# The last 64 rows of a 448-row contraction as two 64-row tiles side by side, in an attention kernel on one core

## The chip, the cores and the metric

The kernel runs on one core of a Trainium2 chip. The metric is the device time of one execution in microseconds, lower is better. A "slot" below is the distance from one matmul's start to the next in an unbroken stream.

## The reference

Two independent attention blocks (A and B) share one form. Each has 16 batches, 144 queries, a model width of 448, 16 heads of width 256, and a key/value cache of 512 positions:

```python
q = (x @ wq).reshape(B, Sq, H, Dh).transpose(0, 2, 1, 3)       # contraction over 448
scores = einsum("bhqd,bhkd->bhqk", q, k_cache) * Dh ** -0.5
p = softmax(scores)
o = einsum("bhqk,bhkd->bhqd", p, v_cache)
out = o.transpose(0, 2, 1, 3).reshape(B, Sq, H * Dh) @ wo
```

One batch and head is a "unit"; there are 2 x 16 x 16 = 512 of them. The contraction of Q is over 448 rows, which is three and a half times the 128 rows of TensorE. That half is what the change is about.

## The kernel before

A Python scheduler issues one step of the pipeline per unit and puts semaphores between the engines. Here are the parts that matter, with cuts marked and short comments added. The fourth chunk of the Q contraction (`kc == 3`) holds 64 rows of zeros, written once, above the 64 rows of real weights, and so runs as a full 128-row matmul.

```python
# PSUM tiles: eight banks in all
qp_ps = ps("qp_ps", [128, 512], F32)                                  # 1 bank: Q of one head, 2 x 144 columns
s_ps = [ps("s_ps%d" % i, [128, 2, 512], F32) for i in range(2)]       # 4 banks: scores, two units in flight
ot_ps = [ps("ot_ps%d" % i, [128, 512], F32) for i in range(2)]        # 2 banks: PV and the row sums
op_ps = ps("op_ps", [128, 512], F32)                                  # 1 bank: output projection
# ... (cut)
def t_q(U):
    pr, b, h = unit(U)
    XG = (pr * Bn + b) // XB
    xsl = XG % NXG
    xo = (b % XB) * SQ
    hg = h // 4

    def e(t):
        ins = None
        for kc in range(4):
            for dc in range(2):
                c0 = h * DH + dc * 128
                ins = t.matmul(qp_ps[:, dc * SQ:(dc + 1) * SQ], lhsT=wq_sb[:, kc, c0:c0 + 128],
                               rhs=xt_sb[:, xsl, kc, xo:xo + SQ], start=(kc == 0 and dc == 0),
                               stop=(kc == 3), skip_group_check=True)
        return ins
    S.add(PE, e, reads=[(("wq", hg), pr), ("wqz", 0), (("xt", xsl), XG)], writes=[("qp", ("q", U))],
          banks=["qp"], name="Q%d" % U)

def t_evac_q(U):
    sl = U % NQT
    src = qp_ps[:, 0:2 * SQ].rearrange("p (c q) -> p c q", c=2)

    def e(v):
        return v.tensor_copy(qt_sb[:, sl, :, :], src)
    S.add(DVE, e, reads=[("qp", ("q", U))], writes=[(("qt", sl), U)], banks=["qp"], name="eq%d" % U)

def t_s(U):
    G, jj = divmod(U, UG)
    ksl = G % NK
    bank = U % 2

    def e(t):
        ins = None
        for c in range(4):
            for dc in range(2):
                ins = t.matmul(s_ps[bank][:, c // 2, (c % 2) * SQ:(c % 2 + 1) * SQ],
                               lhsT=kt_sb[:, 2 * c + dc, (ksl * UG + jj) * 128:(ksl * UG + jj + 1) * 128],
                               rhs=qt_sb[:, U % NQT, dc, :], start=(dc == 0), stop=(dc == 1))
        return ins
    S.add(PE, e, reads=[(("qt", U % NQT), U), (("kt", ksl), G)], writes=[(("sp", bank), U)],
          banks=["s%d" % bank], name="S%d" % U)

def t_exp(U):
    bank = U % 2
    psl = U % NPT

    def e(a):
        return a.activation(pt_sb[:, psl, :, :].rearrange("p (a b) q -> p a (b q)", a=2),
                            s_ps[bank][:, :, 0:2 * SQ], AF.Exp, scale=DH ** -0.5)
    S.add(ACT, e, reads=[(("sp", bank), U)], writes=[(("pt", psl), U)], banks=["s%d" % bank], name="ex%d" % U)

# ... (cut) one step of the main loop; LQ = 6, LS = 2
u = i + LQ
if 0 <= u < NT:
    t_q(u); t_evac_q(u)          # PE: 8 matmuls; DVE: PSUM to SBUF
u = i + LS
if 0 <= u < NT:
    t_s(u); t_exp(u); t_presum(u)  # PE: 8 matmuls; ACT: exp; POOL: sums of exps
u = i
if 0 <= u < NT:
    t_pv(u); t_sum(u)            # PE: 8 + 1 matmuls
    t_recip(u); t_check(u); t_evac_ot(u)   # ACT, DVE, DVE
# ... (cut) then 0 to 12 (once 32) pieces of the output projection, 128x448 matmuls
```

The whole kernel:

## Time and profile before

The time before is 1112.46 us (median of three, 1112.11 to 1113.15).

| quantity | value | view |
|---|---|---|
| PE busy | 1044.0 of 1112.2 us | the page, part 1 |
| slot of a 128x144 matmul | 62.5 ns | timeline: eight take 0.50 us |
| slot of a 128x448 matmul | 188.5 ns | timeline |
| sum of all slots | 12,800 x 62.5 ns + 1,152 x 188.5 ns = 1017 us | worked out |
| PE gaps ahead of Q, waiting for the evacuation | 79 of about 0.27 us, 21 us | single records; waits |
| PE pauses over 1 us after the first matmul | 24.6 us in all | single records |

First the page of the kernel before: its span, its busy times, and some groups. In a group's line the numbers after the bar are busy us, mean ns of one instruction, and idle time before it with what ended it.

```profile
span 1112.2 us, 33041 instructions
...
PE 1044.0 (94%) x13952; PEld 920.7 (83%) x13952; DVE 657.3 (59%) x2183; ACT 620.2 (56%) x1573; POOL 642.2 (58%) x1065
...
L975 ACT ACTIVATE pt_sb<-s_ps 128x576 bf16<-128x576 f32 x512 | 332.9, 650 | 452.2 <-PE s_ps L963 452.1
...
L939 PE MATMUL qp_ps<-xt_sb,wq_sb 128*128 128x144 bf16 x4096 | 346.2, 228 | 52.7 <-DMA wq_sb<-in_A_wq_dram 32.5
...
L951 DVE CAST qt_sb<-qp_ps 128x288 bf16<-128x288 f32 x512 | 225.4, 440 | 101.4 <-PE qp_ps L939 98.0
```

TensorE is the bound. The mean of 228 ns for a matmul is a modelled, pipelined length, not what a matmul costs. That has to be read from the distance between starts. The next lines are the timeline of PE before the change, in a step that carries two pieces of the output projection (start us, length us, then the merged instructions):

```profile
505.39 0.66 PE L939 MATMUL qp_ps<-xt_sb,wq_sb 128*128 128x144 bf16 x8
505.89 0.66 PE L963 MATMUL s_ps<-qt_sb,kt_sb 128*128 128x144 bf16 x8
506.39 0.66 PE L1009 MATMUL ot_ps<-pt_sb,v_sb 128*128 128x144 bf16 x8
```

Eight Q matmuls start at 505.39, the eight of S at 505.89 and the eight of PV at 506.39, so each group takes 0.50 us, or 62.5 ns a matmul. Nothing lies between the groups. In steps without output projection the picture is different:

```profile
70.52 0.23 PE L1021 MATMUL ot_ps<-ps_sb,ones 128*128 128x144 bf16 x1
70.84 0.68 PE L939 MATMUL qp_ps<-xt_sb,wq_sb 128*128 128x144 bf16 x8
```

The row-sum matmul starts at 70.52, so its slot ends at 70.58, but Q starts only at 70.84. Every second Q shows this gap of about 0.26 us. The waits view names its cause (what waited, for whom, total us, times, longest us):

```profile
PE qp_ps L939 <- DMA wq_sb<-in_A_wq_dram: 32.5, 2, 22.7
PEld qp_ps L939 <- DVE qt_sb L951: 26.4, 83, 0.8
PE qp_ps L939 <- DMA wq_sb<-in_B_wq_dram: 9.6, 1, 9.6
...
PE s_ps L963 <- DMA kt_sb<-in_A_k_cache_dram: 3.2, 1, 3.2
```

The Q matmuls of a unit have to wait until DVE has emptied the single Q bank of the unit before. The other lines are the pauses for loads: wq at the start and at the change to block B, and K once.

### The profile page before, as it was taken

How to read it: one execution, taken by the hardware profiler on the slowest of the kernel's cores; microseconds unless marked ns; L12 is line 12 of the kernel's file. 1: busy time of each engine (PE TensorE's matmuls, PEld its weight loads, DVE VectorE, ACT ScalarE, POOL GpSimd, SP SyncE). 2: the span in 40 equal slices, each digit the busy share in tenths (PEclk: the TensorE clock that was granted, in tenths of full speed). 3: DMA queues.
4: the chain of work that ended last, by engine and by line, in shares of the span. 5: the costliest groups of instructions: out<-in, count | busy, mean ns of one | idle time of the engine just before them, and what ended most of it. 6: DMA issues, size and time to landing. Idle time of an engine off the chain costs nothing.

```text
span 1112.2 us, 33041 instructions
## 1 busy us (share of the span) xinstructions
PE 1044.0 (94%) x13952; PEld 920.7 (83%) x13952; DVE 657.3 (59%) x2183; ACT 620.2 (56%) x1573; POOL 642.2 (58%) x1065
## 2 busy tenths in 40 slices
PE   1698999999999999999969999999999999999995
PEld 0597888888888888898858888888888888888884
DVE  1364666666656666666636656666666666666653
ACT  0364555666655555665535555566665555566552
POOL 0364656666656656666636656666665665666652
PEclk9898999999999999999989999999999999999998
DMA  9999999999999999999999999999999999999930
GB/s 251 292 301 304 301 241 273 269 275 287 288 242 263 269 275 258 249 309 277 276 271 313 279 279 280 278 274 269 316 268 271 253 273 285 266 275 259 272 88 12
DMA packets 626399, 294.19 MB, mean 265 GB/s; under 512 B 547776, under 2 KB 555968, under 8 KB 626240
## 3 DMA queue, kind: packets, MB, share of 16 engines
q1 hardware_dynamic: 624512, 287.85, 105.0%
q0 software_dynamic: 1728, 4.13, 1.3%
q8 instruction: 111, 1.82, 0.6%
q14 instruction: 48, 0.39, 0.1%
HBM read 148.90 MB, written 4.13 MB: 138 GB/s over the span
## 4 chain that ended last, share of the span: by engine, by line
PE 76%; DVE 8%; ACT 6%; SPq 4%; DMA 4%; issue 1%; POOLq 0%; POOL 0%; ACTq 0%
PE qp_ps L939 20%; PE s_ps L963 19%; PE op_ps L1100 19%; PE ot_ps L1009 16%; ACT pt_sb L975 4%; SPq L914 3%; DVE run_sb L1065 3%; DVE ring L1052 2%; DVE qt_sb L951 2%; PE ot_ps L1021 2%; DMA kt_sb<-in_A_k_cache_dram 2%; ACT ln_sb L1032 1%; DMA wo_sb<-in_B_wo_dram 1%; DMA wq_sb<-in_A_wq_dram 1%; DMA wq_sb<-in_B_wq_dram 0%
## 5 line engine op out<-in xcount | busy, mean ns | idle before, releaser
L984 POOL TENSOR_TENSOR pp_sb<-pt_sb 128x288 f32<-128x288 bf16 x512 | 373.5, 730 | 415.9 <-ACT pt_sb L975 414.8
L975 ACT ACTIVATE pt_sb<-s_ps 128x576 bf16<-128x576 f32 x512 | 332.9, 650 | 452.2 <-PE s_ps L963 452.1
L1065 DVE TENSOR_REDUCE run_sb<-ot_ps 1x1 bf16<-1x144 f32 x1024 | 262.2, 293 | 342.2 <-ACT ln_sb L1032 342.2
L939 PE MATMUL qp_ps<-xt_sb,wq_sb 128*128 128x144 bf16 x4096 | 346.2, 228 | 52.7 <-DMA wq_sb<-in_A_wq_dram 32.5
L939 PEld LDWEIGHTS qp_ps<-xt_sb,wq_sb 128*128 128x128 bf16 x4096 | 282.8, 99 | 127.2 <-issue 42.8
L963 PE MATMUL s_ps<-qt_sb,kt_sb 128*128 128x144 bf16 x4096 | 343.0, 227 | 3.2 <-DMA kt_sb<-in_A_k_cache_dram 3.2
L1009 PE MATMUL ot_ps<-pt_sb,v_sb 128*128 128x144 bf16 x4096 | 341.7, 227 | 0.0
L951 DVE CAST qt_sb<-qp_ps 128x288 bf16<-128x288 f32 x512 | 225.4, 440 | 101.4 <-PE qp_ps L939 98.0
L963 PEld LDWEIGHTS s_ps<-qt_sb,kt_sb 128*128 128x128 bf16 x4096 | 277.2, 99 | 4.1 <-DMA kt_sb<-in_A_k_cache_dram 3.4
L1009 PEld LDWEIGHTS ot_ps<-pt_sb,v_sb 128*128 128x128 bf16 x4096 | 276.0, 98 | 0.4
L988 POOL TENSOR_TENSOR ps_sb<-pp_sb 128x144 bf16<-128x144 f32 x512 | 250.0, 488 | 40.1
L1100 PE MATMUL op_ps<-wo_sb,ring 128*128 128x448 bf16 x1120 | 264.9, 353 | 1.3 <-DMA wo_sb<-in_B_wo_dram 0.8
L1052 DVE TENSOR_TENSOR ring<-ot_ps,rinv_sb 128x288 bf16<-128x288 f32 (+8 forms) x640 | 231.1, 375 | 0.0
L1037 ACT ACTIVATE rinv_sb<-ln_sb 128x144 f32<-128x144 f32 x512 | 165.4, 323 | 16.2
L1032 ACT ACTIVATE ln_sb<-ot_ps 128x144 f32<-128x144 f32 x512 | 148.6, 290 | 3.2 <-PE ot_ps L1021 3.2
L1100 PEld LDWEIGHTS op_ps<-wo_sb,ring 128*128 128x128 bf16 x1120 | 98.0, 98 | 45.5 <-DMA wo_sb<-in_B_wo_dram 1.2
L1021 PE MATMUL ot_ps<-ps_sb,ones 128*128 128x144 bf16 x512 | 116.1, 227 | 0.0
L1021 PEld LDWEIGHTS ot_ps<-ps_sb,ones 128*128 128x128 bf16 x512 | 50.3, 98 | 0.0
L1118 ACT ACTIVATE ost_sb<-op_ps 128x448 bf16<-128x448 f32 x35 | 18.6, 530 | 8.7 <-PE op_ps L1100 8.6
L1129 POOL DMA_DIRECT2D out_dram<-ost_sb x36 | 20.2, 560 | 4.3 <-ACT ost_sb L1118 4.1
L1100 PE MATMUL qp_ps<-wo_sb,ring 128*128 128x448 bf16 x32 | 7.2, 353 | 0.0
L1100 PEld LDWEIGHTS qp_ps<-wo_sb,ring 128*128 128x128 bf16 x32 | 3.1, 98 | 2.9
(13 smaller groups left out, 6.1 us busy)
## 6 DMA issues: line engine op xcount, KB each, us to landing
v_sb<-in_A_v_cache_dram SPq DMA_DIRECT2D x64, 1024.0 KB, 8.5
v_sb<-in_B_v_cache_dram SPq DMA_DIRECT2D x64, 1024.0 KB, 8.5
out_dram<-ost_sb POOLq DMA_DIRECT2D x36, 112.0 KB, 5.8
wo_sb<-in_A_wo_dram SPq DMA_DIRECT2D x8, 448.0 KB, 9.4
wo_sb<-in_B_wo_dram SPq DMA_DIRECT2D x8, 448.0 KB, 9.4
wq_sb<-in_A_wq_dram SPq DMA_DIRECT2D x4, 768.0 KB, 7.3
wq_sb<-in_B_wq_dram SPq DMA_DIRECT2D x4, 768.0 KB, 8.2
wq_sb<-in_A_wq_dram SPq DMA_DIRECT2D x4, 128.0 KB, 8.1
```

The source lines that it names most:

```text
L939: ins = t.matmul(qp_ps[:, dc * SQ:(dc + 1) * SQ], lhsT=wq_sb[:, kc, c0:c0 + 128], rhs=xt_sb[:, xsl, kc, xo:xo + SQ], start=(kc == 0 and dc ...
L951: return v.tensor_copy(qt_sb[:, sl, :, :], src)
L963: ins = t.matmul(s_ps[bank][:, c // 2, (c % 2) * SQ:(c % 2 + 1) * SQ], lhsT=kt_sb[:, 2 * c + dc, (ksl * UG + jj) * 128:(ksl * UG + jj + 1) ...
L975: return a.activation(pt_sb[:, psl, :, :].rearrange("p (a b) q -> p a (b q)", a=2), s_ps[bank][:, :, 0:2 * SQ], AF.Exp, scale=DH ** -0.5)
L984: return g.tensor_tensor(pp_sb[:, sl, :, :], pt_sb[:, psl, 0:2, :], pt_sb[:, psl, 2:4, :], op=ALU.add)
L988: return g.tensor_tensor(ps_sb[:, sl, :], pp_sb[:, sl, 0, :], pp_sb[:, sl, 1, :], op=ALU.add)
L1009: ins = t.matmul(ot_ps[ob][:, dc * SQ:(dc + 1) * SQ], lhsT=v_sb[:, vsl, j, c * DH + dc * 128:c * DH + (dc + 1) * 128], rhs=pt_sb[:, sl, c, ...
L1021: return t.matmul(ot_ps[ob][:, 2 * SQ:3 * SQ], lhsT=ones[:, :], rhs=ps_sb[:, sl, :], start=True, stop=True)
L1037: return a.activation(rinv_sb[:, sl, :], ln, AF.Exp, scale=-1.0)
L1052: ins = v.tensor_tensor(ring[:, 2 * h:2 * h + 2, r0:r0 + q1 - q0], ot_ps[ob][:, 0:2 * SQ].rearrange("p (c q) -> p c q", c=2)[:, :, q0:q1], ...
L1065: return v.tensor_reduce(run_sb[0:1, k, U:U + 1], ot_ps[ob][0:1, 2 * SQ:3 * SQ], axis=AX.X, op=op)
L1100: ins = t.matmul(acc[0:m, 0:D], lhsT=ring[:, c, col0:col0 + m], rhs=wo_sb[:, c, :], start=(c == first), stop=(c == last))
```

## The change

Its intent is to stop paying a full 128-row slot for 64 rows. The last 64 rows of the weights go to a tile of their own, `wh_sb`: the columns of the first half of each head lie in partitions 0 to 63, those of the second half in partitions 64 to 127. A small DVE copy puts the same 64 rows of x into both halves. Two 64-row matmuls are then to run side by side in the two halves of the array. The Trainium skill (TensorEngine Tiling (Array Packing), Restrictions and Gotchas) says that row tiles cannot use one PSUM bank at the same time. So Q takes two banks, two heads per step, and one evacuation of 576 columns. The bank for that comes from the scores, which go from four banks to three, with an exp for each half.

The diff, cut to its core (cuts marked):

```diff
-        wq_sb = sb("wq_sb", [128, 4, H * DH], BF16)
+        wq_sb = sb("wq_sb", [128, 3, H * DH], BF16)
+        wh_sb = sb("wh_sb", [128, H * 128], BF16)
...
-        qt_sb = sb("qt_sb", [128, NQT, 2, SQ], BF16)
+        qt_sb = sb("qt_sb", [128, NQT // 2, 2, 2 * SQ], BF16)
...
-        qp_ps = ps("qp_ps", [128, 512], F32)
-        s_ps = [ps("s_ps%d" % i, [128, 2, 512], F32) for i in range(2)]
+        qp_ps = ps("qp_ps", [128, 2, 512], F32)
+        s_ps = [ps("s_ps%d" % i, [128, 512], F32) for i in range(3)]
...
+                sem = sems["wq%d" % hg]
+                q.dma_start(wq_sb[:, :, cols], w[0:384, cols].rearrange("(c p) n -> p c n", p=128)).then_inc(sem, 16)
+                wl = w[384:448, cols].rearrange("k (h e n) -> k h e n", e=2, n=128)
+                for dc in range(2):
+                    dst = wh_sb[64 * dc:64 * dc + 64, hg * 512:(hg + 1) * 512]
+                    ins = q.dma_start(dst.rearrange("k (h n) -> k h n", n=128), wl[:, :, dc, :]).then_inc(sem, 16)
+                return ins
+            S.add(SP, e, writes=[(("wq", hg), pr)], dma_sem="wq%d" % hg, n_dma=3, name="wq%d.%d" % (pr, hg))
...
+        def t_xh(XG):
+            sl = XG % NXG
+
+            def e(v):
+                return v.tensor_copy(xt_sb[0:64, sl, 3, :], xt_sb[64:128, sl, 3, :])
+            S.add(DVE, e, reads=[(("xt", sl), XG)], writes=[(("xh", sl), XG)], name="xh%d" % XG)
...
-                for kc in range(4):
+                for j in range(2):
                     for dc in range(2):
-                        c0 = h * DH + dc * 128
-                        ins = t.matmul(qp_ps[:, dc * SQ:(dc + 1) * SQ], lhsT=wq_sb[:, kc, c0:c0 + 128],
-                                       rhs=xt_sb[:, xsl, kc, xo:xo + SQ], start=(kc == 0 and dc == 0),
-                                       stop=(kc == 3), skip_group_check=True)
+                        ro = slice(64 * dc, 64 * dc + 64)
+                        ins = t.matmul(qp_ps[:, dc, j * SQ:(j + 1) * SQ], lhsT=wh_sb[ro, (h + j) * 128:(h + j + 1) * 128],
+                                       rhs=xt_sb[ro, xsl, 3, xo:xo + SQ], start=(j == 0), stop=False,
+                                       skip_group_check=True)
+                for j in range(2):
+                    for dc in range(2):
+                        for kc in range(3):
+                            c0 = (h + j) * DH + dc * 128
+                            ins = t.matmul(qp_ps[:, dc, j * SQ:(j + 1) * SQ], lhsT=wq_sb[:, kc, c0:c0 + 128],
+                                           rhs=xt_sb[:, xsl, kc, xo:xo + SQ], start=False, stop=(kc == 2),
+                                           skip_group_check=True)
                 return ins
-            S.add(PE, e, reads=[(("wq", hg), pr), ("wqz", 0), (("xt", xsl), XG)], writes=[("qp", ("q", U))],
+            S.add(PE, e, reads=[(("wq", hg), pr), (("xt", xsl), XG), (("xh", xsl), XG)], writes=[("qp", ("q", U))],
                   banks=["qp"], name="Q%d" % U)
...
+            for k in range(2):
+                bank = (2 * U + k) % 3
+
+                def e(t, k=k, bank=bank):
+                    ins = None
+                    for c in (2 * k, 2 * k + 1):
+                        for dc in range(2):
+                            ko = (ksl * UG + jj) * 128
+                            ins = t.matmul(s_ps[bank][:, (c % 2) * SQ:(c % 2 + 1) * SQ],
+                                           lhsT=kt_sb[:, 2 * c + dc, ko:ko + 128],
+                                           rhs=qt_sb[:, qsl, dc, qo:qo + SQ], start=(dc == 0), stop=(dc == 1))
                    ...
+                def x(a, k=k, bank=bank):
+                    return a.activation(pt_sb[:, psl, 2 * k:2 * k + 2, :].rearrange("p b q -> p (b q)"),
+                                        s_ps[bank][:, 0:2 * SQ], AF.Exp, scale=DH ** -0.5)
+                S.add(ACT, x, reads=[(("sp", bank), 2 * U + k)], writes=[(("pt", psl), U)], banks=["s%d" % bank],
+                      name="ex%d.%d" % (U, k))
...
-            if 0 <= u < NT:
+            if 0 <= u < NT and u % 2 == 0:
```

For two heads there are then four half matmuls in two pairs and 12 full ones, in place of 16 full ones.

More of the change, by code (lines that the diff above doesn't have):

```diff
@@ L867, in t_init @@
             S.add(ACT, e1, reads=[("scr", 0)], writes=[("scr1", 0)], name="actwarm")
-            def e2(v):
-                return v.memset(wq_sb[0:64, 3, :], 0.0)
-            S.add(DVE, e2, writes=[("wqz", 0)], name="wqz")
             def e4(g):
@@ L881, in e @@
             def e(q):
-                q.dma_start(wq_sb[:, 0:3, cols], w[0:384, cols].rearrange("(c p) n -> p c n", p=128)).then_inc(
-                    sems["wq%d" % hg], 16)
-                return q.dma_start(wq_sb[64:128, 3, cols], w[384:448, cols]).then_inc(sems["wq%d" % hg], 16)
-            S.add(SP, e, writes=[(("wq", hg), pr)], dma_sem="wq%d" % hg, n_dma=2, name="wq%d.%d" % (pr, hg))
+                sem = sems["wq%d" % hg]
[6 more added lines that the diff above has]
+            S.add(SP, e, writes=[(("wq", hg), pr)], dma_sem="wq%d" % hg, n_dma=3, name="wq%d.%d" % (pr, hg))
         def t_load_wo(pr, wg):
@@ L935, in e @@
                 ins = None
-                for kc in range(4):
+                for j in range(2):
                     for dc in range(2):
-                        c0 = h * DH + dc * 128
-                        ins = t.matmul(qp_ps[:, dc * SQ:(dc + 1) * SQ], lhsT=wq_sb[:, kc, c0:c0 + 128],
-                                       rhs=xt_sb[:, xsl, kc, xo:xo + SQ], start=(kc == 0 and dc == 0),
-                                       stop=(kc == 3), skip_group_check=True)
+                        ro = slice(64 * dc, 64 * dc + 64)
[9 more added lines that the diff above has]
+                                           skip_group_check=True)
                 return ins
-            S.add(PE, e, reads=[(("wq", hg), pr), ("wqz", 0), (("xt", xsl), XG)], writes=[("qp", ("q", U))],
+            S.add(PE, e, reads=[(("wq", hg), pr), (("xt", xsl), XG), (("xh", xsl), XG)], writes=[("qp", ("q", U))],
                   banks=["qp"], name="Q%d" % U)
         def t_evac_q(U):
-            sl = U % NQT
-            src = qp_ps[:, 0:2 * SQ].rearrange("p (c q) -> p c q", c=2)
+            sl = U // 2 % (NQT // 2)
             def e(v):
-                return v.tensor_copy(qt_sb[:, sl, :, :], src)
-            S.add(DVE, e, reads=[("qp", ("q", U))], writes=[(("qt", sl), U)], banks=["qp"], name="eq%d" % U)
+                return v.tensor_copy(qt_sb[:, sl, :, :], qp_ps[:, :, 0:2 * SQ])
+            S.add(DVE, e, reads=[("qp", ("q", U))], writes=[(("qt", sl), U // 2)], banks=["qp"], name="eq%d" % U)
         def t_s(U):
@@ L956, in t_s @@
             ksl = G % NK
-            bank = U % 2
-            def e(t):
-                ins = None
-                for c in range(4):
-                    for dc in range(2):
-                        ins = t.matmul(s_ps[bank][:, c // 2, (c % 2) * SQ:(c % 2 + 1) * SQ],
-                                       lhsT=kt_sb[:, 2 * c + dc, (ksl * UG + jj) * 128:(ksl * UG + jj + 1) * 128],
-                                       rhs=qt_sb[:, U % NQT, dc, :], start=(dc == 0), stop=(dc == 1))
-                return ins
@@ L967, in t_s @@
-            S.add(PE, e, reads=[(("qt", U % NQT), U), (("kt", ksl), G)], writes=[(("sp", bank), U)],
-                  banks=["s%d" % bank], name="S%d" % U)
-        def t_exp(U):
-            bank = U % 2
-            psl = U % NPT
-            def e(a):
-                return a.activation(pt_sb[:, psl, :, :].rearrange("p (a b) q -> p a (b q)", a=2),
-                                    s_ps[bank][:, :, 0:2 * SQ], AF.Exp, scale=DH ** -0.5)
-            S.add(ACT, e, reads=[(("sp", bank), U)], writes=[(("pt", psl), U)], banks=["s%d" % bank], name="ex%d" % U)
+            qsl = U // 2 % (NQT // 2)
@@ new lines, in t_s @@
+            qo = U % 2 * SQ
+            psl = U % NPT
+            for k in range(2):
[8 more added lines that the diff above has]
+                                           rhs=qt_sb[:, qsl, dc, qo:qo + SQ], start=(dc == 0), stop=(dc == 1))
+                    return ins
+                S.add(PE, e, reads=[(("qt", qsl), U // 2), (("kt", ksl), G)], writes=[(("sp", bank), 2 * U + k)],
+                      banks=["s%d" % bank], name="S%d.%d" % (U, k))
@@ L979, in t_presum @@
+            for k in range(2):
+                bank = (2 * U + k) % 3
+                def x(a, k=k, bank=bank):
[3 more added lines that the diff above has]
+                      name="ex%d.%d" % (U, k))
         def t_presum(U):
@@ L1092, in t_op_piece @@
             col0 = (r % RS) * 128
-            acc = op_ps if bank == "op" else qp_ps
+            acc = op_ps if bank == "op" else qp_ps[:, 0, :]
             key = "opp" if bank == "op" else "qp"
@@ L1113, in t_evac_op @@
             sl = r % NOST
-            acc = op_ps if bank == "op" else qp_ps
+            acc = op_ps if bank == "op" else qp_ps[:, 0, :]
             key = "opp" if bank == "op" else "qp"
@@ L1220, in bass_concat_heads__mha_block_cached__gqa_block_cached__near_ridge_kernel @@
                 t_store(stores.pop(0)[0])
+            u = i + LQ + 2
+            if 0 <= u < NT and u % (XB * H) == 0:
+                t_xh(u // (XB * H))
             u = i + LQ
-            if 0 <= u < NT:
+            if 0 <= u < NT and u % 2 == 0:
                 t_q(u)
@@ L1227, in bass_concat_heads__mha_block_cached__gqa_block_cached__near_ridge_kernel @@
                 t_s(u)
-                t_exp(u)
                 t_presum(u)
```

## The prediction

> **What bounds it.** TensorE. The page has PE busy 1044.0 of 1112.2 us; its timeline shows why: in a step with two output-projection pieces the Q, S and PV groups of eight 128x144 matmuls start 0.50 us apart (62.5 ns per matmul), each 128x448 matmul takes 0.19 us with nothing between. The sum is 12,800 x 62.5 ns = 800 us plus 1,152 x 0.188 us = 216 us, so 1016 us. The other 96 us: no Q until 22.7 us, a second wait for wq (9.85 us before 53.6), K at 86 us (3.2), program B's wq (9.6, all in the waits), half-clock stretches after those pauses, an 11 us tail, and a repeated gap: in steps without output projection every second Q waits for the DVE to empty its single PSUM bank (waits: PEld on DVE qt_sb, 83 times, 26.4 us; timeline: some 0.25 us of PE each). About 20 us in all. DMA engines look 90% busy, but PE waits for K only once and the queue waits for PE to free K slots (over 700 us), so there is slack.
>
> **What the change does.**
> 1. Q: per two heads 16 full matmuls become 12 full plus 4 half-height ones, in two pairs. If pairs truly overlap, 14 slots: 125 ns saved x 256 = 32 us. The Trainium skill (TensorE: Matmul & The Clock Gate, Part 3) has matmuls of different row tiles start about 4 ns apart; no run here shows it yet.
> 2. It adds 512 changes of tiling mode (into and out of each Q step). The Trainium skill (TensorEngine Tiling, Tiling Modes, Key Properties) says a mode change drains TensorE; no cost given. The trace shows a modelled matmul of 227 ns against a 62.5 ns pitch, so a full drain could expose up to some 165 ns, plus an unhidden weight load (98 ns). My estimate is 70 ns a change: +36 us (0 to 120).
> 3. Q writes its banks every second step only, so the wait for the DVE evacuation should vanish: -20 us.
> 4. DVE: a 576-wide evacuation per pair, estimated at 0.73 us against 2 x 0.44: DVE falls by about 35 us, off the path. ACT: 1,024 exps of 288 at an estimated 0.39 us instead of 512 of 0.65: busy 620 to about 690 us. Off the path.
> 5. Weights: three DMAs per quarter, 256-byte pieces: +1 to 2 us at the start and at program B.
>
> **Sum.** 1112 - 32 - 20 + 36 + 2 = 1098 us. Break-even is at about 100 ns per mode change; below 55 ns it is over 2% faster, above 145 ns over 2% slower. Predicted 1098 us, 8 in 10 between 1068 and 1150; faster 0.44, same 0.31, slower 0.25.
>
> **What would show it.** (1) In the timeline the half matmuls of a pair start only a few ns apart, and a Q step of two heads takes 14 x 62.5 = 0.875 us plus the two changes. (2) The start of the first half matmul after the last matmul before it, and of the first full Q matmul after the last half: each in excess of its pitch. (3) PEld on DVE qt_sb falls from 26.4 us to a few us. (4) Mean durations of the exps and the evacuation; PE waits on ACT stay near nothing. (5) The waits for wq.
>
> **What would make it wrong.** A mode change that costs 150 ns or more (slower); pairs that serialise; nearly free changes (1060 to 1070); steps of uneven length making S wait for an exp or PV for a ring evacuation; waits for K once steps are shorter.

## The result

The changed kernel takes 1116.84 us (median of four, 1116.28 to 1119.25). The ratio to before is 1.0043, with a 95% interval of 1.0026 to 1.0061. The result is correct. 32 us of slots were to go, 20 us of waits were to go, and the kernel became 0.4% slower.

The page after:

```profile
span 1114.5 us, 33472 instructions
...
PE 1052.5 (94%) x13952; PEld 873.0 (78%) x13952; DVE 647.2 (58%) x1934; ACT 669.4 (60%) x2085; POOL 642.2 (58%) x1065
...
L993 ACT ACTIVATE pt_sb<-s_ps 128x288 bf16<-128x288 f32 x1024 | 363.0, 406 | 364.6 <-PE s_ps L982 364.2
...
L965 DVE CAST qt_sb<-qp_ps 128x576 bf16<-128x576 f32 x256 | 192.0, 750 | 153.6 <-PE qp_ps L954 153.6
```

The exps of 288 take 406 ns and the evacuation of 576 takes 750 ns, close to what was predicted (390 and 730). In the waits, those of PEld for the evacuation (DVE qt_sb) have fallen from 26.4 us to 1.1 us, as predicted, and those for loads are a little longer:

```profile
PE qp_ps L947 <- DMA wh_sb<-in_A_wq_dram: 34.6, 3, 21.7
PEld qp_ps L947 <- DVE run_sb L1084: 15.9, 43, 0.4
PE qp_ps L947 <- DMA wh_sb<-in_B_wq_dram: 10.3, 1, 10.3
...
PE s_ps L982 <- DMA kt_sb<-in_A_k_cache_dram: 4.1, 1, 4.1
...
PEld qp_ps L947 <- DVE qt_sb L965: 1.1, 1, 1.1
```

The 43 waits put down to DVE run_sb are new. They are not waits for DVE, which does not hold up those steps: they begin 158 ns after the matmul before, and so do all other steps after a row-sum matmul. They are the first sign of what happened. The time came from the Q step itself. The timeline of PE around one step:

```profile
507.06 0.54 PE L1119 MATMUL op_ps<-wo_sb,ring 128*128 128x448 bf16 x2
507.54 0.30 PE L947 MATMUL qp_ps<-xt_sb,wh_sb 64*128 64x144 bf16 x4
507.77 0.92 PE L954 MATMUL qp_ps<-xt_sb,wq_sb 128*128 128x144 bf16 x12
508.53 0.66 PE L982 MATMUL s_ps<-qt_sb,kt_sb 128*128 128x144 bf16 x8
```

The second of the two output-projection matmuls ends its slot at 507.06 + 2 x 0.1885 = 507.44, and S starts at 508.53. The Q step of two heads thus takes 1.09 us. Before, it took two times 0.50 us. Single records of this step give the starts, in ns from the end of the slot before it:

```
half matmuls    96  100  170  173
full matmuls   328  400  463  525  588 ...  (then every 62.5)
S             1088
```

The two halves of a pair start 3 to 4 ns apart, so they do run side by side. But the first pair starts 96 ns late, the second pair comes after 74 ns and not 62.5, the first full matmul comes 155 ns after the last half one, and the next one after 72 ns. The 74 and the 72 ns belong to the changes too and not to the pairs: half matmuls without partners show the same 74 (e3_half_alone), and a third pair follows the second after 62 ns (e5_three_heads). The weight loads show the same two places:

```profile
507.06 0.10 PEld L1119 LDWEIGHTS op_ps<-wo_sb,ring 128*128 128x128 bf16 x1
507.53 0.11 PEld L947 LDWEIGHTS qp_ps<-xt_sb,wh_sb 64*128 64x128 bf16 x4 [0.37 <-issue]
507.76 0.74 PEld L954 LDWEIGHTS qp_ps<-xt_sb,wq_sb 128*128 128x128 bf16 x12
```

In the stream a weight load runs about 60 ns ahead of its matmul. Here the loads of the half tiles start at 507.53, together with their matmul, and so does the first full load at 507.76. Across a change from 128-row to 64-row matmuls or back, the load starts only 3 to 5 ns before its matmul, in every step after 100 us. The Trainium skill (TensorEngine Tiling (Array Packing), Tiling Modes, Key Properties) says that changing the tiling mode drains TensorE; this trace agrees that a change costs time, and gives the size: 96 ns before the first half matmul on the way in. How much of it is the drain and how much the load that no longer runs ahead, no run here separates. It is 96 ns after a 128x448 matmul (285 ns between starts against 188.5) and after a 128x144 one (158 against 62.5) alike.

### The profile page after: what moved, and what is told of

Read it like the earlier page. It is cut to its first block, busy times and chain, and to the rows that moved or that the text cites. A ratio compares the mean times of both kernels' runs of the same rounds, so it can differ in the third digit from the quotient of the medians.

```text
span 1114.5 us, 33472 instructions
## 1 busy us (share of the span) xinstructions
PE 1052.5 (94%) x13952; PEld 873.0 (78%) x13952; DVE 647.2 (58%) x1934; ACT 669.4 (60%) x2085; POOL 642.2 (58%) x1065
## 4 chain that ended last, share of the span: by engine, by line
PE 90%; SPq 5%; DMA 4%; issue 0%; DVE 0%; ACT 0%; POOLq 0%; POOL 0%; ACTq 0%
PE s_ps L982 22%; PE ot_ps L1028 22%; PE qp_ps L954 19%; PE op_ps L1119 19%; PE qp_ps L947 5%; SPq L922 3%; PE ot_ps L1040 3%; DMA kt_sb<-in_A_k_cache_dram 2%; DMA wo_sb<-in_B_wo_dram 1%; SPq L880 1%; SPq L884 1%; PE qp_ps L1119 0%; DMA wh_sb<-in_A_wq_dram 0%; DMA wh_sb<-in_B_wq_dram 0%; SPq L932 0%
## 5 line engine op out<-in xcount | busy, mean ns | idle before, releaser
L993 ACT ACTIVATE pt_sb<-s_ps 128x288 bf16<-128x288 f32 x1024 | 363.0, 406 | 364.6 <-PE s_ps L982 364.2
L982 PEld LDWEIGHTS s_ps<-qt_sb,kt_sb 128*128 128x128 bf16 x4096 | 282.7, 99 | 32.1 <-issue 4.3
L965 DVE CAST qt_sb<-qp_ps 128x576 bf16<-128x576 f32 x256 | 192.0, 750 | 153.6 <-PE qp_ps L954 153.6
L954 PE MATMUL qp_ps<-xt_sb,wq_sb 128*128 128x144 bf16 x3072 | 241.3, 230 | 0.0
L954 PEld LDWEIGHTS qp_ps<-xt_sb,wq_sb 128*128 128x128 bf16 x3072 | 193.3, 99 | 30.8 <-issue 1.6
L947 PEld LDWEIGHTS qp_ps<-xt_sb,wh_sb 64*128 64x128 bf16 x1024 | 29.4, 94 | 118.5 <-issue 87.6
L947 PE MATMUL qp_ps<-xt_sb,wh_sb 64*128 64x144 bf16 x1024 | 77.4, 230 | 45.7 <-DMA wh_sb<-in_A_wq_dram 34.6
```

Of the source, the lines that this page charges most:

```text
L954: ins = t.matmul(qp_ps[:, dc, j * SQ:(j + 1) * SQ], lhsT=wq_sb[:, kc, c0:c0 + 128], rhs=xt_sb[:, xsl, kc, xo:xo + SQ], start=False, stop=( ...
L965: return v.tensor_copy(qt_sb[:, sl, :, :], qp_ps[:, :, 0:2 * SQ])
L982: ins = t.matmul(s_ps[bank][:, (c % 2) * SQ:(c % 2 + 1) * SQ], lhsT=kt_sb[:, 2 * c + dc, ko:ko + 128], rhs=qt_sb[:, qsl, dc, qo:qo + SQ], ...
L993: return a.activation(pt_sb[:, psl, 2 * k:2 * k + 2, :].rearrange("p b q -> p (b q)"), s_ps[bank][:, 0:2 * SQ], AF.Exp, scale=DH ** -0.5)
```

## The experiments

Seven kernels ran, all correct, each with three timed rounds beside the kernel before (1112.49 us for the first four, 1112.95 us for the last three). The theory to test: (A) the cost is that of the two mode changes in each Q step. The rivals: (B) it comes from the restructuring around the tiles, with exps in halves, two-head steps and fewer score banks; (C) it comes from the pairing, two tiles loading and running at once.

The Q step is measured alike everywhere: from the end of the slot before it to the start of the first S matmul, as the median over the steps after 100 us (the means leave out steps with a pause over 1 us).

| kernel | Q step, ns for two heads | mode changes per step | pauses over 1 us | median time, us | ratio to before |
|---|---|---|---|---|---|
| before | 2 x 500.5 (mean 2 x 541) | 0 | 24.6 us | 1112.46 | 1 |
| after | 1087.5 | 2 | 29.6 us | 1116.84 | 1.0043 |
| e1_full_height | 1000.5 | 0 | 35.1 us | 1097.05 | 0.9852 |
| e2_scores_only | 2 x 500.5 (mean 2 x 541) | 0 | 25.8 us | 1112.54 | 1.0014 |
| e3_half_alone | 1209.5 | 2 | 21.5 us | 1139.01 | 1.0245 |
| e4_two_visits | 1300.5 | 4 | 22.2 us | 1160.19 | 1.0432 |
| e5_three_heads | 1526.5 for three heads | 2 | 36.3 us | 1105.08 | 0.9933 |
| e6_two_banks | 2 x 500.5 (mean 2 x 505) | 0 | 33.6 us | 1094.52 | 0.9831 |
| e7_wq_first | 1000.5 | 0 | 46.8 us | 1103.59 | 0.9909 |

The pauses are the distances over 1 us between the starts of two consecutive matmuls, added up, from the profiled run. Most are waits for loads; in the kernels with two-head steps one of 1.2 us (two in e3_half_alone and e7_wq_first) is a wait for the evacuation in the first steps.

### e1_full_height: the tiling undone, everything else kept

```diff
# in the changed kernel
-        # 4 half matmuls, then 3 full chunks per head and half
-                for j in range(2):
-                    for dc in range(2):
-                        ro = slice(64 * dc, 64 * dc + 64)
-                        ... lhsT=wh_sb[ro, ...], rhs=xt_sb[ro, xsl, 3, ...]
-                        for kc in range(3):
+                        for kc in range(4):
+                            ... lhsT=wq_sb[:, kc, c0:c0 + 128], start=(j == 0 and kc == 0), stop=(kc == 3)
# wq_sb, its loads and the zeroed rows as before; no wh_sb, no copy of x
```

> The changed kernel with only the tiling undone: two heads per Q step, two PSUM banks, three half-unit score banks, but the last 64 rows run as 128-row matmuls over zero rows, as before (16 full matmuls per step). Theory A (mode changes cost more than the slots saved): the Q step goes back to 16 x 62.5 ns = 1.00 us from 1.087 us, 22 us less over 256 steps, while the vanished wait for the evacuation stays vanished: 1091 to 1096 us, over 1% faster than before. Rival B (the restructuring around the tiles eats the gain: exps in halves, wider evacuation, banks): 1115 us or more, since then the 32 us of saved slots are lost too. PE waits on DVE near zero.

Measured: 1097.05 us, ratio 0.9852 (0.9829 to 0.9876). The Q step is back at 16 slots:

```profile
512.58 0.23 PE L1026 MATMUL ot_ps<-ps_sb,ones 128*128 128x144 bf16 x1
512.64 1.16 PE L940 MATMUL qp_ps<-xt_sb,wq_sb 128*128 128x144 bf16 x16
513.64 0.66 PE L968 MATMUL s_ps<-qt_sb,kt_sb 128*128 128x144 bf16 x8
```

From 512.64 to 513.64 is 1.00 us. The tiles cost 1087.5 - 1000.5 = 87 ns a step, or 22 us over 256 steps, and undoing them gave 20 us. Rival B falls: the restructuring without the tiles is a gain. The median lies 1 us above the range of theory A. The trace says why: the pauses for loads grew to 35.1 us from 29.6 us, since the faster steps reach the places earlier where wq and K have not landed.

### e2_scores_only: only the scores moved to three banks

```diff
# in the kernel before
-        s_ps = [ps("s_ps%d" % i, [128, 2, 512], F32) for i in range(2)]
+        s_ps = [ps("s_ps%d" % i, [128, 512], F32) for i in range(3)]
# t_s and t_exp by halves, as in the change; Q as before
```

> The kernel before with only the scores moved to three half-unit banks and exps of 288. Theory A: scores are off the path, 1112 us within 4 us, ACT busy about 670 us, the PE gaps on the Q evacuation (79 gaps of about 0.25 us) still there. Rival B: 1120 us or more, with PE or PEld waiting on ACT.

Measured: 1112.54 us, ratio 1.0014 (0.9989 to 1.0038). The halved exps and the third score bank cost nothing that can be measured, and free a bank. ACT was busy for 696 us, not the expected 670, and PE did not wait for it. The waits for the Q evacuation are still there:

```profile
PEld qp_ps L939 <- DVE qt_sb L951: 26.3, 84, 0.8
```

### e3_half_alone: the mode changes without the pairs

```diff
# in e1_full_height: the last chunk as 64-row matmuls, all in rows 64 to 127
+                for j in range(2):
+                    for dc in range(2):
+                        ... lhsT=wq_sb[64:128, 3, c0:c0 + 128], rhs=xt_sb[64:128, xsl, 3, ...],
+                            start=(j == 0), stop=False
-                        for kc in range(4):
+                        for kc in range(3):
```

> As e1_full_height, but the last chunk of each of the four accumulations is one 64-row matmul on rows 64 to 127, with no partner in the other half. Nothing is saved, two mode changes per step are added. Theory A: the changes alone cost about 200 ns per step, so about 51 us over e1_full_height: 1140 to 1148 us; half matmuls start about 62 ns apart. Rival C (the cost in the changed kernel comes from the pairing, two tiles loading and running at once, not from the change of mode): near e1_full_height, under 1105 us.

Measured: 1139.01 us, ratio 1.0245 (1.0228 to 1.0262). There is the same number of matmuls as in e1_full_height and no two run at once, but two changes per step:

```profile
506.81 0.23 PE L1032 MATMUL ot_ps<-ps_sb,ones 128*128 128x144 bf16 x1
506.97 0.42 PE L939 MATMUL qp_ps<-xt_sb,wq_sb 64*128 64x144 bf16 x4
507.32 0.92 PE L946 MATMUL qp_ps<-xt_sb,wq_sb 128*128 128x144 bf16 x12
508.08 0.66 PE L974 MATMUL s_ps<-qt_sb,kt_sb 128*128 128x144 bf16 x8
```

The slot before ends at 506.87 and S starts at 508.08: 1.21 us against 1.00 us. The two changes cost 209 ns, about 105 ns each, and rival C falls: no pairing is needed for the cost. By single records the parts are about 96 ns before the first half matmul, 11 more before the second, 93 before the first full one and 10 more before the second. The difference from e3_half_alone to the changed kernel, 1209.5 - 1087.5 = 122 ns, is what the overlap of two pairs is worth: two slots, nearly all of the 125 ns that were predicted. The median lies 1 us under the expected range, again through the pauses, which shrank to 21.5 us in the slower kernel.

### e4_two_visits: the same matmuls, twice the changes

```diff
# in the changed kernel: pair of head 0, its six full matmuls, pair of head 1, its six
                 for j in range(2):
                     for dc in range(2):
                         ... half matmuls of head j
-                for j in range(2):
                     for dc in range(2):
                         for kc in range(3):
                             ... full matmuls of head j
```

> The changed kernel with the two pairs of a step visited separately (pair of head 0, its six full matmuls, pair of head 1, its six): the same matmuls, four mode changes per step instead of two. Theory A (about 106 ns per change): 512 more changes, 50 to 55 us over the changed kernel, 1167 to 1172 us. Rivals B and C: within 10 us of the changed kernel.

Measured: 1160.19 us, ratio 1.0432 (1.0415 to 1.0450).

```profile
507.31 0.54 PE L1118 MATMUL op_ps<-wo_sb,ring 128*128 128x448 bf16 x2
507.78 0.24 PE L947 MATMUL qp_ps<-xt_sb,wh_sb 64*128 64x144 bf16 x2
507.95 0.55 PE L953 MATMUL qp_ps<-xt_sb,wq_sb 128*128 128x144 bf16 x6
508.43 0.24 PE L947 MATMUL qp_ps<-xt_sb,wh_sb 64*128 64x144 bf16 x2
508.60 0.55 PE L953 MATMUL qp_ps<-xt_sb,wq_sb 128*128 128x144 bf16 x6
508.99 0.66 PE L981 MATMUL s_ps<-qt_sb,kt_sb 128*128 128x144 bf16 x8
```

The step grew by 1300.5 - 1087.5 = 213 ns for two more changes, about 106 ns each, which is 54 us over 256 steps. The time grew by 43 us, less than expected: 7 us of the difference are pauses for loads that shrank from 29.6 us to 22.2 us. Most of the rest lies just behind the pauses: there 128x144 matmuls start 120 ns apart instead of 62.5 for a while (the granted clock was 0.50 from 53.6 to 56 us here). Outside the half tiles the changed kernel's trace has 168 such distances and this one 104, which is 3.7 us less.

### e5_three_heads: fewer changes

```diff
# in the changed kernel
-            if 0 <= u < NT and u % 2 == 0:
+            if 0 <= u < NT and u % 3 == 0:
                 t_q(u)
# t_q: three pairs, then 18 full matmuls (432 of 512 columns of each bank); qt_sb of three groups of three heads
```

> The changed kernel with three heads per Q step in the same two banks (432 of 512 columns): 342 mode changes instead of 512, the same pairs. Theory A: a step of three heads saves three slots (188 ns) and still pays about 212 ns for its two changes, plus some 8 ns for the third pair, so it costs about 1.53 us against 1.50 us without tiles: about 16 us under the changed kernel, 1098 to 1104 us, still not under e1_full_height (1097 us). Rival B (restructuring, not the number of changes): not faster than the changed kernel, 1116 us or more.

Measured: 1105.08 us, ratio 0.9933 (0.9908 to 0.9959), so 12 us faster than the changed kernel, and 1 us outside the range of theory A.

```profile
511.34 0.54 PE L1121 MATMUL op_ps<-wo_sb,ring 128*128 128x448 bf16 x2
511.82 0.36 PE L948 MATMUL qp_ps<-xt_sb,wh_sb 64*128 64x144 bf16 x6
512.11 1.30 PE L955 MATMUL qp_ps<-xt_sb,wq_sb 128*128 128x144 bf16 x18
513.25 0.66 PE L984 MATMUL s_ps<-qt_sb,kt_sb 128*128 128x144 bf16 x8
```

The slot before ends at 511.34 + 2 x 0.1885 = 511.72 and S starts at 513.25. A step of three heads takes 1526.5 ns; without tiles it would take 24 x 62.5 = 1500 ns. Three pairs nearly pay for their two changes, but not quite. Once more the pauses took part of the gain: 36.3 us against 29.6 us.

### e6_two_banks: the freed bank without tiles

```diff
# in e2_scores_only
-        qp_ps = ps("qp_ps", [128, 512], F32)
+        qp_ps = [ps("qp_ps%d" % i, [128, 512], F32) for i in range(2)]
# t_q and t_evac_q use qp_ps[U % 2], one head per step; the tail of the output projection uses qp_ps[0]
```

> The kernel before with the scores in three half-unit banks (same time as before in e2_scores_only) and the freed bank used as a second Q bank: one head per step, alternating banks, no tiles, evacuations of 288 as before. If the gain of e1_full_height is the missing wait for the Q evacuation: the 79 to 84 PE gaps of 0.25 us vanish, 1091 to 1098 us. If it is the wider steps or the single wide evacuation that pays: 1105 us or more.

Measured: 1094.52 us, ratio 0.9831 (0.9815 to 0.9848), the lowest time, though its interval overlaps that of e1_full_height. Both beat the kernel before and the changed one. The gaps are gone: 79 of them (21.3 us) before, one of 0.2 us now. In a step without output projection Q now starts one slot after the row-sum matmul:

```profile
67.65 0.23 PE L1024 MATMUL ot_ps<-ps_sb,ones 128*128 128x144 bf16 x1
67.72 0.66 PE L939 MATMUL qp_ps<-xt_sb,wq_sb 128*128 128x144 bf16 x8
```

So the gain beneath the tiles comes from the second Q bank, and needs neither two-head steps nor the wide evacuation. The page:

```profile
span 1094.0 us, 33719 instructions
...
PE 1028.2 (94%) x13952; PEld 920.6 (84%) x13952; DVE 657.5 (60%) x2183; ACT 696.5 (64%) x2085; POOL 642.6 (59%) x1065
```

### e7_wq_first: a miss

```diff
# in e1_full_height: a wq load goes ahead of the K load of its wave where it need not wait longer than that one
+                for gg in range(g, g + m):
                     ...
+                    if glw < HG and (gg < 2 or gg > 2) and wlo <= max(s_min, UG * (g + m - NK) - LS):
+                        plan(t_load_wq, prw, glw)
                         ...
                 plan(t_load_k, g, m)
```

> e1_full_height with the loads of wq put ahead of the K loads that they need not wait for. e1_full_height has 35 us of PE pauses over 1 us on loads of wq and K (before: 25 us), among them 11.9, 5.1 and 9.3 us before Q steps. Theory: part of its gain is lost there and is to be had back: the pauses at 540 and 561 us shrink to under 3 us each, 1080 to 1090 us. Rival: the queue is bound by bytes there, and the pause only moves to K: 1094 us or more.

Measured: 1103.59 us, ratio 0.9909 (0.9886 to 0.9933), 7 us slower than e1_full_height. The first Q started at 10.8 us and not at 21.5 us, but the waits moved to K, as the rival said. These are the waits of e1_full_height, and then those of e7_wq_first:

```profile
PE qp_ps L940 <- DMA wq_sb<-in_A_wq_dram: 35.2, 3, 21.5
...
PE s_ps L968 <- DMA kt_sb<-in_A_k_cache_dram: 5.1, 1, 5.1
```

```profile
PE s_ps L968 <- DMA kt_sb<-in_A_k_cache_dram: 22.4, 7, 13.1
...
PE qp_ps L940 <- DMA wq_sb<-in_A_wq_dram: 16.0, 2, 10.8
```

In all the pauses after the first Q grew to 46.8 us from 35.1 us, which by itself takes back the earlier start; the rest are shorter waits and slow stretches behind them. This other order of the same loads is no gain. What order would be best is left open.

## Why the prediction was wrong

The sign was wrong (1.3% faster was predicted, 0.4% slower measured), although the time lay in the range. The terms of its sum, one by one:

1. "-32": right. The pairs run side by side, 3 to 4 ns apart, as the Trainium skill (TensorE: Matmul & The Clock Gate, Part 3) says of row tiles, and e3_half_alone against the changed kernel puts the saving at 122 ns a step (31 us).
2. "My estimate is 70 ns a change: +36 us (0 to 120)": this is the step that failed. The mechanism was right (each change costs time, and the weight load is no longer hidden) and the size was off. A change measured 105 ns (e3_half_alone, 209 ns for two) and 106 ns (e4_two_visits, 213 ns for two more), so the term is 512 x 105 ns = 54 us. The prediction had put the break-even at about 100 ns, and the cost lies just beyond it.
3. "-20": right, and a little small. The gaps ahead of Q came to 21.3 us and went; e6_two_banks shows that the second bank does it. Four more such waits stood in the first steps of the kernel before (880 ns between starts against the 120 ns of that stretch, 3 us in all), and are gone too: 24 us together.
4. Exps and evacuation off the path: right (e2_scores_only, no difference; e1_full_height, with the wide evacuation too, is faster than before). The evacuation group fell by 33 us (225.4 to 192.0), while DVE's busy time fell by 10 us only, as neighbouring DVE instructions overlap in the trace: its groups add up to more than its busy time.
5. "+1 to 2 us at the start and at program B": too small. The pauses grew by 5 us: the largest new one is 3.1 us for a part of wh near the start, and 1.2 us is the one wait for the evacuation that is left.

With the measured terms: 1112 - 31 - 24 + 54 + 5 = 1116 us, against 1116.84 us measured.

"There is slack" in the loads was half right: in the middle PE hardly waits for them, but at the start and at the change to block B the loads are late, and a faster kernel waits longer there (24.6 us before, 33.6 us in e6_two_banks, 21.5 us in the slower e3_half_alone). Between kernels that differ in the step alone, a seventh to a third of the difference was absorbed in that way (7 of 54 us from the changed kernel to e4_two_visits, 8 of 24 us from e2_scores_only to e6_two_banks).

## What to carry to other kernels

Row tiles do overlap, but a visit to them pays for two mode changes, here 209 to 214 ns, with one, two or three pairs (each counted as one slot) or four single tiles in between; with 144 columns a pair saves about 61 ns, so a visit needs four pairs or more before it pays (an estimate from these runs; three pairs were still 26 ns short). When a change bundles several things, undo each by itself: here the part meant as preparation, a PSUM bank freed from the scores and given to Q, was worth 1.7% alone, and the tiles spent it. And when TensorE is the bound, cost a matmul by the distance between starts, then look at what those distances are at the seams.

## What the Trainium skill lacked or had wrong

- TensorEngine Tiling (Array Packing), Key Properties, says that a change of tiling mode drains TensorE, without a size. Here the first half matmul starts 96 ns late, after 128x144 and 128x448 matmuls alike, and a pair of changes costs 209 to 214 ns in all, with no weight load running ahead across either.
- The same page's table of theoretical speedup ("Up to 2×" for a contraction of up to 64) does not say how many matmuls a visit must hold. Here two pairs lost 87 ns a visit and three lost 26 ns.
- TensorE: Matmul & The Clock Gate, Part 3, gives about 4 ns between the starts of tiles; that agrees (3 to 4 ns). It does not say how pairs follow each other: here the second pair after a change comes 74 ns after the first (as do single half matmuls in e3_half_alone), and the third 62 ns after the second, as close as full matmuls of the same 144 columns.
- Trainium Kernel Development and Optimization, Best Practices, prefers the busy share of weight loads, beside the share of peak FLOPs, to that of matmuls as a measure. The half on matmuls agrees: PE shows 94% in the kernel before, in the slower changed one and in the fastest one. The other half holds only in part: PEld shows 83%, 78% and 84% there, but 80% in e5_three_heads, which is faster than the kernel before; with half tiles that load side by side it doesn't rank the kernels.
